# Linear attention and a mixture of experts on one core: the first batch's loads and steps in a new order

## The chip, the core and the metric

The kernel runs on one core of a Trainium2 chip. A core has a matrix engine (TensorE, PE in the profile, with PEld for its weight loads), VectorE (DVE), ScalarE (ACT), GpSimd (POOL) and SyncE (SP). Each engine works through its own list of instructions in order and waits on semaphores for the others. Transfers from memory are issued by SP, ACT or POOL and carried by 16 DMA engines: queue 1 in the profile holds what SP issues, queue 10 what ACT issues, queue 0 what POOL issues. The metric is device time in microseconds (us) of one execution; the figure compared is the median of several runs.

## What is computed

Linear attention over 8 batches of 8 heads, 576 tokens and head size 64, and then a mixture of 4 experts over the 4608 tokens:

```
phi(x) = where(x > 0, x, exp(x) - 1) + 1
kv  = einsum('bhsd,bhde... over s', phi(k), v)        # 64 x 64 per head
z   = sum over s of phi(k)
x   = (phi(q) @ kv) / (phi(q) . z + 1e-6)             # heads side by side: 4608 x 512
p   = domain_probs / (sum of domain_probs + 1e-9)     # 4608 x 4
out = sum over e of p[:, e] * (relu(x @ w1[e]) @ w2[e])   # w1[e]: 512 x 1024, w2[e]: 1024 x 512
```

All inputs are float32 in memory; the matrix products run on float16.

## The kernel before

**Tiles.** The tokens are cut into nine tiles of 512. Tile j below 8 holds the first 512 tokens of batch j; the ninth collects the 64 tokens left over in each batch. For each tile the attention makes x, which is transposed to xT, and then four experts follow, each with a layer 1 (x times w1, relu) and a layer 2 (times w2, scaled by p and added up in `acc`). The products are done in a form that saves multiplications (`Block` and `layer2_product`, with sums of weights, of tokens and of hidden values made on DVE and POOL). Only expert 0 of tile 0 is done plainly, by `layer1_half` and `layer2_part`.

**Batch 0.** Its attention stands at the start of the kernel, when nothing else can run, and has a class of its own, `First` (lines 558 to 666). Its k and v come in four pieces of two heads (288 KB each), its q in four pieces of 256 KB: pieces 0 and 1 are the first token half, pieces 2 and 3 the second half, of heads 0 to 3 and 4 to 7. In memory a row of a q piece is 512 bytes long, a row of a k or v piece 2304 bytes. The steps, by the names that the order uses, with i the number of the piece:

- `lq`, `lk`, `lv`: loads, issued on SP or ACT as the settings `LQ`, `LK`, `LV` say; `lpr0`: the first probabilities
- `ke`, `kl`, `km` (lines 582 to 590): exp of k on ACT, max(k + 1, 1) on the engine that `KL` names, their minimum on DVE; `qe`, `ql`, `qm` (lines 599 to 607): the same for q
- `vc` (line 593): v cast to float16 on the engine that `VC` names
- `kv` (line 626): 18 matmuls on PE and two copies of the result, on engines that `KC` names
- `qT` (line 615): four transposes of q on PE and a copy on ACT
- `nd` (line 648): numerators and denominators on PE, a reciprocal and a product on DVE; the first digit is the pair of head pairs, the second the token half
- `xT` (line 662): two transposes of x on PE and a copy on ACT or DVE; first digit the pair of heads, second the token half
- `L` (line 675): layer 1 of expert 0 for two of the eight column blocks and one token half, in two parts (heads of pairs 0 and 1, then of pairs 2 and 3)
- `warm` (line 1016): matmuls on zeros, whose result nobody reads; `WARM` has their numbers

**Weights and batch 1.** They are loaded by POOL (`load_second`), which converts weights to float16 on the way: `w100` is layer 1, expert 0, piece 0, and so on; `k0`, `v2`, `q1` are pieces of batch 1, `rk0`, `rv1` its leftover tokens. The sums of weights are `s` and `t`, the sums of tokens `ts`, the products of the later experts `p1` to `p7`, `c22` and `y`.

**The order.** Nothing is scheduled by the machine. Each step is a generator that records its instructions; the list `EARLY` (lines 103 to 135) is read from left to right and each name advances its step by one part. Instructions go to the lists of their engines in the order in which they are recorded. What comes after `EARLY` runs by positions in other settings. `BANK` says which pair of PSUM banks a step uses, and so which earlier step has to be done with it. Raw pieces of q, and of batch 1, share six buffers (`praw`, line 220). A transfer also waits until the one that used its semaphore before has landed.

Of the kernel before, what the change touches and what calls it, by code (L numbers as in the profile page):

```python
# [90 lines left out]
    "LK": 'ASSS',  # L91
    "LV": 'SSSS',
    "KL": 'VVVV',
    "VC": 'PVAP',
    "QL": 'VVPV',
    "QT": 'AAAA',
    "KC": ('AA', 'AV', 'VA', 'AA'),
    "XT": ('AA', 'AA', 'AV', 'AV'),
    "CUT": (((0, 2, 4),) * 4, ((0, 2, 4),) * 4),
    "MOVE": {"m73.10": 512.0, "m73.11": 512.0, "m73.20": 512.0, "m73.21": 512.0, "m72.41": 528.0},  # L100
    "WARM": (14, 3, 2, 1, 5),
    "BANK": {'qT0': 'py', 'qT1': 'b', 'nd00': 'py', 'nd00+': 'b', 'kv2': 'py', 'xT00': 'b', 'kv3': 'b', 'nd10+': 'b', 'L00': 'b', 'L10': 'py', 'nd01': 'b', 'xT01': 'py', 'nd11+': 'b', 'L20': 'e', 'L30': 'e', 'L01': 'e', 'L11': 'py', 'L21': 'py', 'L31': 'b', 'b1.qT3': 'py', 'b1.nd30': 'py', 'b1.nd21': 'b', 'b1.q1': 'b', 'b1.qT1': 'py', 'b1.nd01': 'py', 'b1.xT2': 'b', 'b1.nd11': 'py', 'b1.xT0': 'b'},
    "EARLY": (
        "lq2 lq3 lq0 lk0 qe0 ql0 ql3 qm0 kl0 lk1 lpr0 ke0 km0 qe2 ql2 qm2 lv0 ke1 kl1 km1 warm0 qT0 lv1 lk2 qe3 qm3 warm1 qT2 qT0 vc0 w100 warm2 kv0 vc1 qT2",
        "warm3 kv1 lk3 kv0 kv0 kl2 kv1 kl3 w102 kv1 nd01 lv3 nd01 warm4 xT11 xT01 ke2 km2 qT3 w103 vc3 lv2 ke3 vc2 nd00 w101 km3 xT01 w110 xT11 w111 kv3 k3 kv2",
        "qT3 lq1 nd00 qe1 xT00 w200 kv3 rk1 ql1 kv3 kv2 w201 qm1 L01 kv2 nd11 xT10 L31 qT1 v0 nd11 rv0 xT00 xT10 L10 xT21 rk0 xT21 v1 xT31 L11 qT1 xT31 nd10",
        "L01 L01 rv1 L31 w120 nd10 ts0.2 L00 ts0.0 xT30 ts0.1 xT20 L31 s0.0 L20 xT20 L30 xT30 L10 L10 L00 L00 L30 ts0.3 L30 p1.011 s1.0 p1.010 L11 L20 p1.010",
        "p2.010 s1.1 L20 w121 p2.010 p1.011 L21 L21 L21 s1.2 p6.010 p5.010 w210 L11 s1.3 p6.011 y0.30 p2.011 p6.010 p7.010 w211 p7.010 s0.1 p6.011 c22.010 v2",
        "y0.31 y0.00 p4.010 p2.011 y0.32 y0.33 p5.011 b1.k3 k0 pr0 y0.33 t0.0 t0.1 b1.km3 p7.011 p7.011 c22.011 y0.01 y0.02 y0.03 p4.010 b1.lk y0.20 y0.03 k2",
        "p4.011 s0.2 p3.010 p4.011 p3.011 y0.21 y0.10 y0.22 p3.010 y0.11 b1.v0 q1 k1 p1.021 y0.23 p1.021 p3.011 p1.020 s2.0 y0.12 v3 p2.021 b1.lv p1.020 t0.3",  # L110
        "s2.1 p2.020 s2.3 s2.2 y0.23 b1.v1 q0 t0.2 p6.020 p6.020 y0.13 p6.021 y0.13 y1.20 p7.020 y1.21 p2.020 p5.020 p7.020 w130 p2.021 y1.22 y1.23 t1.0 y1.10",
        "w131 p5.021 b1.v2 q3 b1.lkm y1.11 p6.021 b1.k0 b1.k2 b1.k1 w220 t1.1 t1.2 p7.021 y1.12 p7.021 c22.020 p3.020 y1.23 b1.v3 b1.km0 p4.020 p4.020 y1.00",
        "y1.01 q2 w221 y1.13 p4.021 b1.km2 b1.km1 b1.kv c22.021 p3.021 y1.02 y1.03 p1.030 p4.021 b1.q1 y1.30 y1.13 b1.load1 p1.031 b1.q0 p3.020 y1.31 p3.021",
        "p1.030 b1.qm1 b1.qT1 y1.32 y1.03 b1.qm0 s3.0 p1.031 w231 b1.qT0 s3.1 p2.030 y1.33 p6.030 b1.kv b1.qT0 p6.031 p2.031 b1.nd00 b1.nd01 b1.q3 p6.030 s3.3",
        "y1.33 p7.030 b1.loadlq p2.030 p5.030 b1.qm3 b1.qT3 p6.031 p7.030 w230 b1.qT1 b1.nd01 p7.031 p4.030 b1.qT3 s3.2 c22.030 b1.nd10 b1.nd11 b1.nd00 p2.031",
        "p3.030 b1.nd11 b1.nd10 p7.031 y2.00 y2.01 b1.nd30 p5.031 p4.031 p4.030 b1.next b1.nd31 b1.nd30 y2.20 b1.load0 b1.xT0 b1.lq b1.lqm b1.nd31 b1.q2 b1.qm2",
        "y2.21 b1.xT3 y2.02 c22.031 p4.031 b2.load2 y2.03 s0.3 b1.xT3 b1.qT2 y2.22 y2.23 b2.load1 b1.xT1 b1.load4 b1.load3 b1.load2 lpr b1.qT2 b1.nd20 p3.031",
        "b1.xT1 p3.030 b1.nd21 y2.03 b1.xT0 b1.nd20 b1.nd21 y2.23 y2.10 y2.11 ts1.0 p1.101 p1.101 b1.load5 t1.3 b2.load0 t2.0 b1.xT2 y2.12 y2.13 b1.xT2 b2.k1",
        "ts1.1 y2.30 y2.31 p1.100 p1.100 y2.32 y2.33 p3.031 p2.101 y3.20 y2.13 b2.km1 p6.100 b2.lk p2.100 t3.0 b2.load4 p2.101 p6.101 p6.100 p2.100 b2.lv",
        "ts1.2 p7.100 ts1.3 p7.100 b2.k0 y3.21 p5.100 y2.33 y3.22 t2.1 p4.100 y3.23 p6.101 p5.101 p4.100 p7.101 y3.30 c22.100 p3.100 b2.ones b1.qTl b2.v3 y3.00",  # L120
        "y3.01 p7.101 p4.101 b2.k2 b2.lkm y3.23 b2.km0 b2.load3 c22.101 b2.v1 y3.31 p3.100 t2.3 y3.32 p4.101 hs10.00 p3.101 b2.load5 y3.02 p1.110 b2.km2 y3.33",
        "p3.101 y3.03 b2.k3 b2.v0 b2.km3 b2.v2 b2.kv p1.110 y3.33 b2.load10 m10.21 b2.load7 p1.111 y3.03 y3.10 hs10.01 b1.qTl b2.q0 y3.11 p6.110 hs10.10",
        "hs10.02 y3.33 pr1 y3.12 y3.03 p1.111 m10.21 b2.q3 b2.load11 b2.qm0 y3.13 m10.51 hs10.11 p2.110 p6.111 p6.110 b2.q2 p2.111 m10.51 b2.qm3 y3.13 p2.110",
        "p6.111 t2.2 p7.110 m10.11 p5.110 m10.20 p7.110 b2.qm2 m10.11 b2.q1 c22.110 hs10.03 hs10.12 p7.111 m10.61 b2.qm1 t3.1 m10.20 p4.110 p4.110 p3.110",
        "p3.110 m10.50 p1.120 t3.2 b1.nl p2.111 p5.111 b3.load1 hs10.13 m10.61 m10.31 m10.31 m10.50 m10.10 p7.111 p4.111 b2.kv hs11.00 m10.10 m10.71 p1.120",
        "c22.111 t3.3 p6.120 m10.71 b2.lq b2.lqm p4.111 m10.60 b1.nl hs11.01 p3.111 p1.121 p6.120 y3.13 b2.load6 b2.qT m10.41 b2.qTl m10.60 m10.30 p2.120",
        "b2.nd1 p3.111 m10.41 m10.30 p7.120 b2.nd1 b2.nd0 hs11.10 y3.23 m10.70 m10.70 m11.21 hs11.11 p2.120 p5.120 m11.21 m10.40 p7.120 p4.120 hs11.03 p1.121",
        "p6.121 m11.20 m11.51 c22.120 p3.120 m10.40 b2.nd0 m11.20 p4.120 b3.k1 m11.50 m11.51 b3.km1 m11.11 p6.121 p2.121 m11.50 b2.nd1 b2.nd2 p3.120 p7.121",
        "m11.11 b2.nd3 b2.nd2 p1.130 hs11.02 p7.121 hs12.00 p2.121 b3.load0 b2.nd3 hs11.13 m11.10 m11.10 b2.next m11.61 m11.61 p5.121 p1.130 c22.121 p2.130",
        "m11.60 m11.31 p3.121 p6.130 m11.31 p4.121 b2.nd3 p6.130 hs11.12 m11.71 p4.121 p3.121 hs12.01 hs12.02 p2.130 m11.60 b2.nd4 hs12.10 p7.130 m11.71",  # L130
        "hs12.12 b2.nd5 p7.130 b2.nd2 b2.load8 m11.30 p5.130 p1.131 p1.131 m11.41 ts2.0 b2.nd4 b2.nd5 b2.nd5 m11.30 m11.41 m11.70 hs12.03 p6.131 p6.131 m12.20",
        "m11.70 m11.40 hs12.11 b3.ones c22.130 p4.130 p3.130 b1.xl p7.131 m12.21 p4.130 p7.131 m12.20 m11.40 b2.nl p2.131 b3.v0 p1.200 m12.21 b2.nl m12.50",
        "p2.131 m12.50 m12.51 p4.131 hs12.13 m12.51 ts2.1 p3.130 m12.10 m12.10 m12.11 m12.11 p5.131 p1.200 ts2.3 m12.60 m12.61 ts2.2 m12.60 b3.k0 m12.61",
        "c22.131 hs13.00 b2.load9 p4.131 p6.200",
    ),
}

# [1032 lines left out]
```

## Time and profile before

| what | value |
|---|---|
| median of 3 runs | 485.64 us (484.6 to 485.81) |
| the profiled execution | 484.06 us, of which the span of the core's instructions 482.3 us |
| TensorE busy | 474.5 us (98%) |
| VectorE, ScalarE, GpSimd busy | 377.6, 331.4, 356.1 us |
| granted TensorE clock | 1.0 |
| bytes moved by DMA | 53.67 MB, mean 111 GB/s |
| the same up to 60 us, in slices of 12 us | 218 to 292 GB/s |

The span runs from the first to the last instruction of the program. Busy time counts an engine as busy while an instruction of its own runs; matmuls are pipelined, so their ends overlap the next one's start. A chain is the work that ended last, followed back step by step to what released it. The time from issue to landing of a transfer includes its wait behind others. In a line of a stretch of time the columns are: the stretch, its length, busy time and number of instructions of PE, PEld, DVE, ACT and POOL, the granted clock, the busy share of the DMA engines, and GB/s.

### The profile page before, as it was taken

What the parts mean: (1) busy time and instruction counts of PE and PEld (TensorE: products, weight loads), DVE (VectorE), ACT (ScalarE), POOL (GpSimd) and SP (SyncE); (2) the same over time, 40 slices, a digit from 0 to 9 for tenths busy, and PEclk for the clock granted to TensorE, in tenths of its full rate; (3) what the DMA queues carried; (4) which work ended last, traced back from release to release, by engine and by line L of the source; (5) the groups of instructions that cost most, each with busy time, mean ns of one, the idle gap of its engine ahead of it and who ended that gap; (6) DMA issues with size and microseconds to landing.
All of it is one profiled execution on the core that took longest, in us unless ns stands there. A gap on an engine that the chain in (4) does not pass through costs nothing.

```text
span 482.3 us, 12013 instructions
## 1 busy us (share of the span) xinstructions
PE 474.5 (98%) x4565; PEld 407.4 (84%) x4565; DVE 377.6 (78%) x794; ACT 331.4 (69%) x662; POOL 356.1 (74%) x340
## 2 busy tenths in 40 slices
PE   7999999999999999999999999999999999999997
PEld 3766766898889888998889888988898888888886
DVE  5778988997868895889679885988787756775677
ACT  4689989956895599649874888478954465446540
POOL 5566044789866986789777977697769877987775
PEclk9999999999999999999999999999999999999999
DMA  8999986442445154533552436323230020003002
GB/s 292 219 218 256 232 212 210 124 112 83 135 140 115 39 160 154 119 59 117 173 134 62 112 123 170 78 73 112 65 68 12 2 88 2 0 1 89 2 1 87
DMA packets 80025, 53.67 MB, mean 111 GB/s; under 512 B 45088, under 2 KB 72736, under 8 KB 79968
## 3 DMA queue, kind: packets, MB, share of 16 engines
q1 hardware_dynamic: 69920, 40.56, 30.6%
q0 software_dynamic: 8800, 11.27, 12.1%
q10 hardware_dynamic: 1248, 1.08, 0.7%
q8 instruction: 35, 0.57, 0.5%
q14 instruction: 22, 0.18, 0.1%
HBM read 45.16 MB, written 9.44 MB: 113 GB/s over the span
## 4 chain that ended last, share of the span: by engine, by line
PE 96%; DVE 1%; DMA 1%; issue 0%; ACT 0%; SPq 0%; DVEq 0%
PE py L830 39%; PE pb L887 25%; PE pe L887 19%; PE py L735 6%; PE ph L675 1%; PE psum_nd L492 1%; PE psum_kv L464 1%; DMA rawq<-in_q_dram 1%; PE pb L830 1%; PE pe L830 1%; DVE kpos L586 0%; PE psum_nl L510 0%; PE psum_num L648 0%; PE psum_xh L662 0%; DVE qp L607 0%
## 5 line engine op out<-in xcount | busy, mean ns | idle before, releaser
L726 DVE SCALAR_TENSOR_TENSOR acc<-py,p_sb,acc 128x256 f32<-128x256 f32 (+1 forms) x382 | 182.3, 489 | 42.3 <-PE py L830 38.3
L871 DVE CUSTOM_DVE_ANT_0 h<-pe,u 128x512 f16<-128x512 f32 x140 | 96.2, 689 | 45.5 <-PE pe L887 27.8
L887 PEld LDWEIGHTS <-w 128*128 128x128 f16 x1120 | 108.9, 98 | 16.2
L797 POOL TENSOR_TENSOR hs<-h 128x512 f16<-128x512 f16 x64 | 74.6, 1165 | 56.9 <-DVE h L871 52.8
L830 PEld LDWEIGHTS <-h 128*128 128x128 f16 x1024 | 99.6, 98 | 11.5
L830 PE MATMUL py<-w,h 128*128 128x256 f16 x744 | 106.4, 273 | 0.0
L898 ACT COPY u<-pb 128x512 f32<-128x512 f32 x140 | 82.5, 592 | 29.9 <-PE pb L887 27.8
L799 POOL TENSOR_TENSOR hs<-hs,h 128x512 f16<-128x512 f16 x64 | 73.9, 1155 | 26.3 <-PE py L830 23.8
L887 PEld LDWEIGHTS <-s 128*128 128x128 f16 x840 | 81.2, 98 | 12.0 <-DVE s L767 0.2
L887 PE MATMUL pb<-tt,w 128*128 128x256 f16 x560 | 83.9, 273 | 0.0
L830 PEld LDWEIGHTS <-hs 128*128 128x128 f16 x768 | 74.5, 98 | 8.8 <-issue 0.2
L803 POOL TENSOR_TENSOR hs<-h,hs 128x512 f16<-128x512 f16 x64 | 74.4, 1162 | 0.9 <-PE py L830 0.7
L830 PE MATMUL py<-t,hs 128*128 128x256 f16 x496 | 74.1, 273 | 0.0
L801 POOL TENSOR_TENSOR h<-h 128x512 f16<-128x512 f16 x64 | 73.9, 1154 | 0.1
L920 ACT ACTIVATE h<-pe 128x512 f16<-128x512 f32 x70 | 42.0, 601 | 41.3 <-PE pe L887 40.7
L913 ACT COPY pe<-pb 128x512 f32<-128x512 f32 x70 | 40.0, 572 | 42.0 <-PE pb L887 15.8
L941 ACT ACTIVATE h<-pb 128x512 f16<-128x512 f32 x70 | 41.9, 601 | 6.0 <-PE pb L887 5.9
L887 PE MATMUL pe<-tt,s 128*128 128x256 f16 x280 | 42.0, 273 | 0.0
L887 PE MATMUL pb<-tt,s 128*128 128x256 f16 x280 | 41.8, 273 | 0.0
L887 PE MATMUL pe<-xT,s 128*128 128x256 f16 x248 | 37.1, 273 | 0.0
L887 PE MATMUL pb<-xT,w 128*128 128x256 f16 x248 | 37.1, 273 | 0.0
L830 PE MATMUL py<-w,hs 128*128 128x256 f16 x248 | 37.0, 273 | 0.0
(132 smaller groups left out, 594.4 us busy)
## 6 DMA issues: line engine op xcount, KB each, us to landing
w<-in_moe_w_dram POOLq DMA_DIRECT2D x14, 512.0 KB, 10.6
out_dram<-acc SPq DMA_DIRECT2D x28, 256.0 KB, 2.6
rawb<-in_k_dram SPq DMA_DIRECT2D x24, 256.0 KB, 3.0
rawb<-in_q_dram SPq DMA_DIRECT2D x24, 256.0 KB, 2.7
rawb<-in_v_dram SPq DMA_DIRECT2D x24, 256.0 KB, 2.7
out_dram<-acc SPq DMA_DIRECT2D x12, 128.0 KB, 2.4
w<-in_moe_w_dram POOLq DMA_DIRECT2D x4, 256.0 KB, 5.5
rawb<-in_k_dram POOLq DMA_DIRECT2D x4, 256.0 KB, 10.4
```

The lines of the kernel that those rows point to most:

```text
L726: nc.vector.scalar_tensor_tensor(out=acc, in0=ps, scalar=pscal, in1=acc, op0=AO.mult, op1=AO.add)
L797: nc.gpsimd.tensor_tensor(out=hs[0], in0=a21, in1=a22, op=AO.add)
L799: nc.gpsimd.tensor_tensor(out=hs[1], in0=hs[0], in1=a11, op=AO.subtract)
L801: nc.gpsimd.tensor_tensor(out=a21, in0=a11, in1=a21, op=AO.subtract)
L803: nc.gpsimd.tensor_tensor(out=hs[3], in0=a12, in1=hs[1], op=AO.subtract)
L830: nc.tensor.matmul(out=ps, lhsT=lhsT(k), rhs=rhs[:, k], start=first and k == 0, stop=k == FH - 1, skip_group_check=True,)
L871: nc.vector._custom_dve(TENSOR_ADD_SAT, out=out, in0=ps, in1=u, s0=BIG, s1=0.0)
L887: nc.tensor.matmul(out=ps[:, kk], lhsT=lk(kc), rhs=rhs[:, kc], start=first and kk == 0 and kc == 0, stop=kc == 1, skip_group_check=True,)
L898: nc.scalar.copy(u, self.b)
L913: nc.scalar.copy(self.e5, self.b)
L920: nc.scalar.activation(self.h[:, :, 0, 0:NH], self.e5, AF.Relu)
L941: nc.scalar.activation(self.h[:, :, 1, 0:NH], self.b, AF.Relu)
```

## The change

Only settings change; no function does.

- SP's list of loads was q2, q0, k1, probabilities, v0, v1, k2, k3, v3, v2, q1. It becomes q2, v0, k1, v1, k2, v2, k3, v3, q0, q1, probabilities. ACT issues q3 and k0 as before.
- POOL had max(q + 1, 1) of piece 2, the casts of v0 and v3, and issued the first piece of w after the cast of v0. Now it casts v0, issues `w100`, casts v1 and issues `w102`, `w103`, `w101` and the rest. All four max(q + 1, 1) are on DVE, the casts of v2 and v3 on ACT.
- ACT and DVE begin with q pieces 2 and 3 and then k; q pieces 0 and 1 come after k is done.
- Layer 1 of expert 0 began with column blocks in both token halves. Now the second token half is begun in all column blocks (`L01 L11 L31 L21`) before the first half of the tokens.
- PSUM banks of the steps of batch 0 are given out anew; the warm matmuls are 21 and not 25.
- The rest of `EARLY`, up to tile 1, has the same steps in a new order; weights and batch 1's pieces are loaded in nearly the order of before, with the pieces of batch 1 at other places among them.

```diff
-    "VC": 'PVAP',
-    "QL": 'VVPV',
+    "VC": 'PPAA',
+    "QL": 'VVVV',
     "QT": 'AAAA',
-    "KC": ('AA', 'AV', 'VA', 'AA'),
+    "KC": ('AA','AV','VA','AA'),
     "XT": ('AA', 'AA', 'AV', 'AV'),
...
-    "WARM": (14, 3, 2, 1, 5),
-    "BANK": {'qT0': 'py', 'qT1': 'b', 'nd00': 'py', 'nd00+': 'b', 'kv2': 'py', 'xT00': 'b', 'kv3': 'b', 'nd10+': 'b', 'L00': 'b', 'L10': 'py', 'nd01': 'b', 'xT01': 'py', 'nd11+': 'b', 'L20': 'e', 'L30': 'e', 'L01': 'e', 'L11': 'py', 'L21': 'py', 'L31': 'b',
+    "WARM": (13, 3, 2, 1, 2),
+    "BANK": {'qT3': 'py', 'kv1': 'py', 'nd01': 'py', 'kv3': 'py', 'xT11': 'py', 'nd11': 'py', 'xT31': 'py', 'nd00': 'py', 'qT1': 'py', 'xT10': 'py', 'nd10': 'py', 'xT30': 'py', 'L01': 'e', 'L11': 'e', 'L21': 'b', 'L31': 'b', 'L00': 'e', 'L10': 'e', 'L20': 'b', 'L30': 'b',
...
     "EARLY": (
-        "lq2 lq3 lq0 lk0 qe0 ql0 ql3 qm0 kl0 lk1 lpr0 ke0 km0 qe2 ql2 qm2 lv0 ke1 kl1 km1 warm0 qT0 lv1 lk2 qe3 qm3 warm1 qT2 qT0 vc0 w100 warm2 kv0 vc1 qT2",
-        "warm3 kv1 lk3 kv0 kv0 kl2 kv1 kl3 w102 kv1 nd01 lv3 nd01 warm4 xT11 xT01 ke2 km2 qT3 w103 vc3 lv2 ke3 vc2 nd00 w101 km3 xT01 w110 xT11 w111 kv3 k3 kv2",
-        "qT3 lq1 nd00 qe1 xT00 w200 kv3 rk1 ql1 kv3 kv2 w201 qm1 L01 kv2 nd11 xT10 L31 qT1 v0 nd11 rv0 xT00 xT10 L10 xT21 rk0 xT21 v1 xT31 L11 qT1 xT31 nd10",
-        "L01 L01 rv1 L31 w120 nd10 ts0.2 L00 ts0.0 xT30 ts0.1 xT20 L31 s0.0 L20 xT20 L30 xT30 L10 L10 L00 L00 L30 ts0.3 L30 p1.011 s1.0 p1.010 L11 L20 p1.010",
...
+        "lq2 lv0 lq3 lk0 lk1 lv1 qe2 qe3 lk2 lv2 ql3 ql2 vc0 w100 vc1 qm3 qm2 warm0 lk3 ke0 qT2 warm1 kl0 lv3 w102 km0 kl1 w103 qT2 ke1 w101 w110 w111 rv0 kv0",
+        "qT3 km1 qT3 kv0 kv0 ke2 warm2 kv1 kl2 kv1 ke3 vc2 vc3 kv1 kl3 km2 nd01 w200 nd01 warm3 rv1 w201 k1 rk0 kv2 k2 w120 k3 xT11 xT01 lq0 lq1 qe0 ql0 km3",
+        "ql1 qm0 kv2 warm4 kv3 rk1 lpr0 w121 w210 v2 k0 w211 v0 v1 v3 q1 qe1 kv2 xT11 kv3 kv3 xT01 nd11 q2 w130 qm1 qT1 qT0 L01 L11 qT1 w131 w220 q0 qT0 w221",
+        "nd11 nd00 xT21 L31 xT31 L21 nd00 q3 xT21 xT31 nd10 xT00 xT10 L21 L01 xT10 L21 xT00 nd10 xT30 L31 xT20 xT30 L01 L11 L30 xT20 L30 L20 L20 L10 L10 L00",
...
```

(The lines of the list that follow, up to tile 1, have the same steps in another order; it ends with the same steps.)

## The prediction

> **What bounds the kernel now.** I read the page first (span, busy time, slices, chain), then busy time by stage, then the chain of the first 20 us, then the DMA queues stretch by stretch. From the page:
>
> ```profile
> span 482.3 us, 12013 instructions
> PE   7999999999999999999999999999999999999997
> ...
> PE 96%; DVE 1%; DMA 1%; issue 0%; ACT 0%; SPq 0%; DVEq 0%
> ```
>
> TensorE (PE) is the bound. Busy time by stage (us, then PE, PEld, DVE, ACT, POOL, granted clock, DMA share, GB/s) says where it is not:
>
> ```profile
> 8.00:12.00 4.00, 2.71 (x49) 1.42 (x48) 3.90 (x8) 2.81 (x8) 3.98 (x6) 1.00 1.09 367
> 12.00:16.00 4.00, 2.99 (x62) 2.04 (x62) 3.20 (x9) 3.17 (x8) 4.00 (x7) 1.00 1.24 205
> 16.00:20.00 4.00, 4.00 (x52) 3.54 (x53) 2.75 (x9) 2.09 (x8) 1.91 (x3) 1.00 1.15 212
> 20.00:60.00 40.00, 40.00 (x346) 29.03 (x344) 33.43 (x66) 36.31 (x74) 15.84 (x22) 1.00 1.18 236
> 60.00:480.00 420.00, 418.71 (x4043) 369.06 (x4041) 331.08 (x698) 283.98 (x565) 327.36 (x294) 1.00 0.34 93
> ```
>
> From 16 us on PE never rests. So the change is worth what it does to one moment, the start of that unbroken stretch at 15.98 us, provided no hole appears behind it. What sets that moment, from the chain (start, us, what):
>
> ```profile
> 1.25 4.94 DMA rawq<-in_q_dram
> ...
> 6.22 0.64 ACT ee L601
> ...
> 11.12 1.24 DVE kpos L586 x2
> ...
> 15.23 0.70 DVE x_sb L652
> ...
> 15.98 0.28 PE psum_xh L662 x2
> ```
>
> A q piece landing at 6.20 lets ACT and DVE begin; they carry the chain to the x that PE transposes at 15.98. DMA, the third resource, is full from the start. First query, 8.3 to 11.4 us: queue 1 holds SP's loads. Second, 8.3 to 9.2: the first piece of w, 4.9 us to landing. Third, 52 to 54: POOL's queue 0 beside queue 1.
>
> ```profile
> q1 hardware_dynamic: 889, 1.19, 105.6%
> ```
>
> ```profile
> w<-in_moe_w_dram POOLq DMA_DIRECT2D x1, 256.0 KB, 4.9
> ```
>
> ```profile
> q0 software_dynamic: 310, 0.36, 94.0%
> q1 hardware_dynamic: 309, 0.08, 28.8%
> ```
>
> Until 11.4 us queue 0 moves nothing, though w is issued from 8.38: in this kernel the first loads and w hardly meet. When both queues have work (310 packets against 309, and 90 against 87 in 49.5 to 50.5) they take turns packet by packet, whatever the sizes.
>
> **The parts.**
>
> *Fewer warm matmuls* (25 to 21): they stand before waits, worth nothing. The clock matters: the first twelve take up to 634 ns, from 5.9 us on 376 to 393.
>
> *Earlier start.* q pieces 2 and 3 feed ACT and DVE first; piece 2 lands at 4.25, not 6.20 (SP's first load, issued 0.74, 3.5 us). Behind them the loads have the same bytes, so I keep the landings' spacing of 0.75 us per 288 KB and 0.65 per 256 KB: k0 and v0 6.1, k1 6.85, v1 7.6, k2 8.35, v2 9.1, k3 9.85, v3 10.6, q0 11.25, q1 11.9. Adding rows down ACT's list (exp 0.62 to 0.67, the next starting 0.55 later; qT copies 0.60; kv copies 0.21; v casts 0.66): k exp 6.15, copies of kv0 end 8.9, that of kv1 9.66, k exp 3 ends 10.55, v casts 11.65, q exps 12.75. Down DVE's (q lin and min 0.42, k lin 0.45 to 0.68, reciprocal 0.21, norm 0.69): kv1's copy 9.9, k min 2 11.0, first x 11.85, q lin 12.25, k min 3 12.65, then the lin of q1.
>
> *From there everything hangs on q1.* DVE's list is: lin q1, min q0, copy kv2, min q1; ACT's: exp q1, copy kv2, xT, two copies of kv3, xT, two qT copies. PE's next steps (numerators of pairs 2 and 3, two turns, then layer 1) wait for those. If q1 can be used at T: kv2 copied T+1.25, last kv3 copy T+1.95, numerators T+2.0, turn of q0 T+2.4, layer 1 T+2.6, and 0.13 lost before the next numerators, which wait for the last qT copy at T+3.55. At T+2.4 the same 1.57 us of small matmuls is left as before at 15.98 (6 transposes of x at 0.11, 2 numerators at 0.34, a turn at 0.23). So the change is T + 2.53 − 15.98 = T − 13.45, with T at least 12.55, when DVE gets there. With q1 at 11.9 it is −0.9.
>
> *The POOL queue is the catch.* Before, POOL does a q lin (1.92 us from 4.33) and a v cast at 7.76, and issues w at 8.38. After, its list is cast v0, w, cast v1, w, w, w: v0 lands at 6.1, the cast takes 0.66, so w is issued at 6.8, 1.6 us earlier, while v3, q0 and q1 still queue (before, q1 was ahead of w). First packet of w: 3.0 us after the issue as before gives 9.8; a newcomer behind large packets takes longer (SP's k load issued at 44.52: no packet of queue 1 before 48.1, 3.6 us), which gives 10.4; with half a us more, 10.9. I take 10.4: the engines then hold large packets too. From then on a q packet goes with each packet of w. q pieces are 512 packets of 512 B, 32 per engine; a pair takes 2 us × 16 / 310 = 0.103 us, against 0.02 for a q packet alone (0.65/32). At 10.4 some 57 are left, 5.9 us: q1's data ends at 16.3, T = 16.7 with the 0.35 from last packet to landing. Bounds: w at 9.8 leaves 64 and part of v3, T = 17.75; at 10.9 about 40, T = 15.1. w has four pieces of 16 packets per engine in that stretch, so the pairing doesn't run dry.
> [...]
>
> *Price:* T − 13.45 = +3.25 (+1.6 to +4.3).
>
> *Later order.* w comes in nearly the same order and DMA stays full, so landings move little. Counting PE's work on from layer 1 at T+2.6, the second half of w2 of expert 2 is needed 41.9 us later. It landed at 58.8 before (need 60.4); one q piece (0.65) now comes after it: 58.15. With T = 16.7 the need is at 61.2: no wait. With T = 12.55 it is at 57.0: 1.15 us of wait that takes the gain back. The probabilities' 8 KB go from fourth to last on SP; the first py is scaled some 14 us after layer 1 begins, which covers them. SP now issues q1 into the buffer of q piece 2, after that one's exp and lin; those end by 5.5, and SP is at q1 no sooner than 6.1, when k0, whose semaphore it also waits for, lands. On POOL, batch 1's k pieces 1 and 2 go ahead of w1 of expert 2 (0.65 each): it lands near 32.9 and is needed 19.1 us after layer 1 begins, 34.2 at the earliest. Casts and banks are charged nothing: DVE 33.4 and ACT 36.3 of 40 us (20 to 60) have room for what moves: a v cast from POOL to ACT (0.66), a q lin from POOL to DVE (0.42) against a v cast from DVE to POOL (0.75); without that cover they cost up to 1.1.
>
> **Sum.** The profiled execution took 484.06 us, span 482.3 and 1.76 around it; the runs' median, 485.64, is 1.58 above it. 484.06 + 3.25 = 487.31; as a median, 488.9. A change below 0.3% (1.46 us) can't be told from none.
>
> **The rivals.**
>
> *A. q delayed by w, clock kept:* 488.9 (487.2 to 490.0). Against it: no row shows w starting while SP's queue is full; w's first packet at 11.4 comes just as SP's loads end, which also fits a newcomer that stands behind all of them.
>
> *B. The same, and PE's clock falls.* PE would do kv3 at about 14.5 and nothing until 18.3. Before, its longest idle stretch once warm is 0.77 us. Cold, the first 4.7 us (1.2 to 5.9) ran at half rate; again, that costs 2.35: 491.2. [...] No row here shows a fall within the kernel.
>
> *C. w stays behind all SP loads as before* (not slower). T = 12.55, −0.9, 484.7. Place: the DMA engines at 9.8 to 11; it decides if T stays under 13.45. With the wait for w2 it is +0.2: 485.8. If w also streams 1.6 us earlier the wait is gone and the gain stays, at most some 1.6 with my walk off by 0.7.
>
> *D. Partial sharing,* T from 13 to 14.9: −0.45 to +1.45, 486.1.
>
> **Numbers.** A 0.45, B 0.13, C 0.28, D 0.14. Slower: A, B and a little of D, 0.60. Faster by over 0.3% only in the best of C, raised a little for errors in my walk, 0.12. The rest 0.28. Predicted is A's 488.9, its own range 487.2 to 490.0. The range goes from C's 484.7 to B's 491.2, leaving out C's better end and B's worse.
>
> **What would show it.** In the changed kernel: w first issued near 6.8; queue 1 sharing packets with queue 0 from about 10.4; q0 and q1 landing near 13.4 and 16.7, the latter 10 us after its issue and not 5; ACT's exp of q1 and DVE's lin waiting for that DMA; PE dense from about 19, none of it waiting for w. Wrong if q1 lands near 12 (C), if matmuls of layer 1 start 0.22 us apart instead of 0.11 (B), or if PE waits for DVE or ACT between 20 and 110 us, where the order is new and many of its inputs were ready only 0.05 to 0.3 us ahead.

## The result, and the profile after

The changed kernel takes 490.0 us (median of 6 runs, 489.35 to 490.43) against 484.34 us for the kernel before, measured beside it (483.96 to 485.81): a ratio of 1.0108, interval 1.009 to 1.0125. The profiled execution took 489.61 us, with a span of 487.8 us against 482.3 before.

From the page of the changed kernel, the span, TensorE's slices, the granted clock in slices, and the shares of the chain:

```profile
span 487.8 us, 12000 instructions
...
PE   7899999999999999999999999999999999999997
...
PEclk9799999999999999999999999999999999999999
...
PE 90%; DMA 4%; ACT 2%; DVE 2%; issue 1%; ACTq 0%; SPq 0%; DVEq 0%
```

PE is still the bound, but its second slice (12 to 24 us) is no longer full, the granted clock has a 7 in that slice where full speed is 9, and the chain holds 4% of DMA (20 us) where it held 1%.

Busy time by stage shows the clock more closely. The stretches are cut to where the clock changes in the changed kernel (columns: stretch, length, PE, PEld, DVE, ACT, POOL, granted clock, DMA share, GB/s). First the changed kernel, then the same cut of the kernel before, whose matmuls come up to full speed at the same 5.9 us:

```profile
5.90:9.30 3.40, 3.14 (x52) 1.59 (x51) 2.90 (x6) 2.58 (x6) 2.96 (x5) 1.00 1.05 402
9.30:12.70 3.40, 1.54 (x36) 1.10 (x31) 2.29 (x7) 3.31 (x7) 3.40 (x6) 1.00 1.15 287
12.70:16.10 3.40, 2.19 (x29) 1.31 (x28) 1.91 (x6) 1.59 (x6) 2.13 (x3) 0.51 1.28 211
16.10:19.60 3.50, 3.50 (x33) 3.00 (x31) 0.90 (x2) 1.37 (x3) 1.35 (x2) 0.51 1.16 211
19.60:23.00 3.40, 3.40 (x42) 2.85 (x41) 2.82 (x8) 1.56 (x5) 0.71 (x1) 1.00 1.14 216
```

```profile
5.90:9.30 3.40, 2.01 (x14) 0.79 (x13) 2.98 (x7) 3.08 (x6) 1.90 (x3) 1.00 1.05 404
9.30:12.70 3.40, 2.13 (x48) 1.26 (x46) 3.19 (x7) 2.21 (x7) 3.38 (x6) 1.00 1.13 316
12.70:16.10 3.40, 3.07 (x63) 2.12 (x63) 2.71 (x7) 2.58 (x7) 3.40 (x6) 1.00 1.24 205
```

From 9.3 to 12.7 us PE is busy for 1.54 of 3.40 us (45%) and right behind that the clock is halved for 6.8 us; before, it was busy for 2.01 us (59%) in the stretch from 5.9 and for 2.13 us (63%) in this one, and the clock stayed. Counted from the moment at which the warm matmuls come up to full speed (5.91 us), the changed kernel's clock falls 6.83 us later, at 12.73, and comes back after another 6.83, at 19.56; in experiment 6 the two times are 6.83 and 3.42, in experiment 7 about 3.4 and 10.2. All are close to whole multiples of 3.41, and a stretch of that length, counted from that moment, is called a window below. No stretch of 3.4 us is empty: PE's longest pause behind 2 us is 1.21 us, and that one, the wait for q1, comes at 14.5, when the clock is down already. The first matmuls of layer 1 are the slowed ones (changed kernel, timeline; start, duration, engine, line, what):

```profile
17.12 1.92 PE L675 MATMUL ph<-xT,w 128*128 128x256 f16 x8
```

Eight take 1.92 us with the end of the last, and 1.04 us at full speed (experiment 8, below). The chain, which counts from start to start, has 1.71 us for eight here and 0.87 for eight from 21.34 on: 0.21 apart against 0.11.

The delay at the start is in the chain of the first 18 us of the changed kernel (start, duration, what):

```profile
1.26 4.84 DMA kraws<-in_k_dram
...
6.21 7.83 DMA rawq<-in_q_dram
...
14.50 0.14 DVE qp L607
...
15.31 0.38 ACT xT L664
...
17.33 0.85 PE ph L675 x4
```

q1, issued at 6.21, lands at 14.05, 7.83 us later, and everything up to layer 1 hangs on it. Its neighbour on the queue, q0, lands at 11.28, undisturbed. POOL's issue is the other side (timeline), and the queues from 11 to 13 us show them together (packets, MB, share):

```profile
6.35 0.87 POOL L244 DMA_DIRECT2D w<-in_moe_w_dram  x1
```

```profile
q0 software_dynamic: 280, 0.27, 80.4%
q1 hardware_dynamic: 379, 0.17, 40.2%
```

Asking for w 2 us sooner brought nothing: it lands at 13.44, before at 13.30.

Behind 20 us PE waits again, in places that had no wait before. The waits of PE from 20 us on (us in total, times, longest), and a piece of the chain from 78 to 106 us:

```profile
PE py L830 <- ACT acc L724: 0.9, 2, 0.5
PE py L830 <- DVE acc L726: 0.4, 1, 0.4
```

```profile
82.05 4.88 DMA rawb<-in_q_dram
86.95 0.63 ACT qp L364
```

A q piece of batch 2, which SP now issues at 82.05 (the same piece before: 78.03), lands at 86.9, and ACT, which works through its list in order, stands for 0.70 us until then.

To see where the 5.5 us of span went, I add up from each moment on the matmuls still to be done at full speed, warm ones left out, in both traces. The changed kernel is behind by 1.9 us at 20 us, 2.65 at 60, 3.7 at 90, 4.9 at 120 and 5.6 at the end: a third in the head, the rest in several smaller steps behind it. The experiments take these apart.

### The profile page after: what moved, and what is told of

Its sections match the earlier page's. It is cut to its first block, busy times and chain, and to the rows that moved or that the text cites. A ratio compares the mean times of both kernels' runs of the same rounds, so it can differ in the third digit from the quotient of the medians.

```text
span 487.8 us, 12000 instructions
## 1 busy us (share of the span) xinstructions
PE 478.0 (98%) x4561; PEld 409.0 (84%) x4561; DVE 377.4 (77%) x794; ACT 332.8 (68%) x663; POOL 354.6 (73%) x339
## 3 DMA queue, kind: packets, MB, share of 16 engines
q0 software_dynamic: 8800, 11.27, 11.9%
## 4 chain that ended last, share of the span: by engine, by line
PE 90%; DMA 4%; ACT 2%; DVE 2%; issue 1%; ACTq 0%; SPq 0%; DVEq 0%
PE py L830 37%; PE pb L887 24%; PE pe L887 18%; PE py L735 5%; DMA rawq<-in_q_dram 2%; PE ph L675 2%; PE psum_nd L492 1%; DMA rawb<-in_q_dram 1%; DMA kraws<-in_k_dram 1%; PE psum_kv L464 1%; PE pb L830 1%; DVE acc L726 1%; DMA xT<-x_sb 1%; PE pe L830 1%; DVE h L871 1%
```

## The experiments

Ratios are to the kernel before, measured beside each: 484.74 us in experiments 1 to 4, 484.58 in 5 to 8, 484.39 in 9 and 10. Kernel 3 is the kernel of experiment 3, and so on.

**1. w asked for after v1's cast.** One entry of the list, changed kernel:

```diff
-... lv2 ql3 ql2 vc0 w100 vc1 qm3 qm2 warm0 ...
+... lv2 ql3 ql2 vc0 vc1 w100 qm3 qm2 warm0 ...
```

> The changed kernel with one swap on POOL: the cast of v1 ahead of the first piece of w, so that w is issued near 8.4 us as before and not at 6.35. Theory A (the last q loads are slowed by w, which takes turns with them): q1 lands near 12.0 instead of 14.05, and PE begins layer 1 near 15.2 instead of 17.1. Rival K (only the fallen clock costs, the late q1 is harmless): q1's landing may move, the time does not. For the whole both have a part: the clock fell at 12.7 because of the idle time between 9.3 and 12.7, which this edit does not touch, so it should fall here too, and PE then does up to 4 us of dense work at half rate. Expected: q1 at 12.0 in the trace, clock 0.5 from 12.7 to 16.1 or 19.6; time 0 to 1.5 us below the changed kernel's 490.0.

Measured 488.65 us, 1.0076 (1.0064 to 1.0089). w is issued at 8.48, q1 lands at 12.03 and not at 14.05, w at 13.34. So the mixing is the cause of q1's delay, but not of the fallen clock. The profiled execution, 487.42, was the fastest of five, and in it the clock never fell; the other four (488.33 to 488.79) have mean clocks of 0.992 to 0.996. Same instructions, other outcome. PE's busy time in the stretch before the danger point, with the clock full from 6.85 us in this execution:

```profile
10.27:13.68 3.41, 2.12 (x47) 1.30 (x46) 3.11 (x9) 2.94 (x6) 3.41 (x5) 1.00 1.22 255
```

2.12 of 3.41 us (62%), and the clock holds. Yet the same trace, cut from 9.32 to 12.74 us as the window lay in the changed kernel, has only 1.56 of 3.42 us (46%). In the twelve profiled executions of this case the warm matmuls come up to full speed at anything from 4.5 to 7.2 us, and the windows, counted from there, lie at other moments of the kernel accordingly. That this made the difference among the five is my reading; where the windows lay in the other four was not recorded.

**2. More warm matmuls**, w left early. 34 in place of 21, the new ones around kv2 and kv3:

```diff
-    "WARM": (13, 3, 2, 1, 2),
+    "WARM": (13, 3, 2, 3, 4, 2, 7),
...
-... rk0 kv2 k2 ... kv2 warm4 kv3 rk1 ...
+... rk0 kv2 warm5 k2 ... kv2 warm4 kv3 warm6 rk1 ...
```

> The changed kernel with 12 more matmuls on zeros in the idle time of PE before layer 1 (3 instead of 1 before kv2, 2 after it, 4 instead of 2 before kv3, 7 after it), w issued early as in the changed kernel. Theory K: the granted clock stays 1.0 between 12.7 and 19.6, and 1.3 to 1.8 us of the 5.6 go: 488.4. q1 still lands near 14. Rival (the clock's fall lay beside waiting and cost nothing): clock 1.0 and 490.0. [...]

Measured 487.73, 1.0069 (1.0056 to 1.0083): 2.3 us under the changed kernel although q1 lands even later, at 14.26. The clock is 0.999 to 1.0 in all five executions. At 20 us this kernel is 0.81 us behind the kernel before, where the changed kernel is 1.9 behind; so 1.1 of the 2.3 us are saved in the head itself, and the rest in waits behind it.

**3. Both.** The step of 1, and warm matmuls (13, 3, 2, 3, 3, 2, 4) in the places of 2.

> Both edits: w after the cast of v1, and 8 more matmuls on zeros. If A and K together are all of the loss up to 30 us, PE's unbroken stretch begins as early as my sum for an undisturbed start had it (0.9 us ahead of before), and the time is 2.6 to 3.3 us below the changed kernel, near 487.0; what is left over before's 484.3, some 2.7 us, then lies behind 60 us. If the time is near 484, the later losses were only consequences of the head.

Measured 486.43, 1.0036 (1.0023 to 1.0048). Against 2 that is 1.3 us less, the price of the mixed queues (it also has four warm matmuls fewer). Against 1 it is 2.2 us less, of which the clock explains about half: 1's one execution with the clock up took 487.42, still 1.0 above. In that execution the late q piece of batch 2 takes 5.52 us to land (4.82 here, below), and PE waits 1.05 us behind it where it waits 0.35 here; why it takes longer is not shown. With q1 at 12.00 the head is 0.3 us ahead of the kernel before at 20 us by the sum of what is left, and yet the kernel ends 1.7 us later than it: something behind the head costs 2 us. Its chain still has the late q piece:

```profile
79.69 4.82 DMA rawb<-in_q_dram
84.53 0.63 ACT qp L364
```

**4. The kernel before up to 68 us, the changed order behind.** The first 396 entries of the list are those of the kernel before, and what is left comes in the changed kernel's order; all other settings are those of before.

> The kernel before, its first 396 entries of the order (to some 68 us), then the changed kernel's order for all later entries. Theory L (the new order behind 68 us costs by itself: ACT waits at 82 us for a q piece of batch 2): 2 to 3 us above before, 486.3 to 487.3, with PE gaps between 80 and 120 us. Rival (those gaps come from what the changed head left late): within 0.5 us of before, 484.3.

Measured 485.85, 1.0025 (1.0017 to 1.0034). The late order costs 1.1 us by itself. In its profiled execution, the fastest of eleven, PE has no wait between 20 and 95 us and two holes behind, at 100.78 and 115.68. The waits of PE from 20 us on:

```profile
PE pb L887 <- ACT h L941: 0.4, 1, 0.4
PE py L830 <- DVE acc L726: 0.4, 1, 0.4
```

**5. The converse.** Kernel 3 up to 68 us (398 entries), then the order of before.

> The head, and everything up to about 68 us, in the changed kernel's order, with w asked for after v1's cast and the extra warm matmuls (as in the run that measured 486.43); from there the order of the kernel before. Theory: about 1.1 us of the loss belongs to the late part of the order (the q piece of batch 2 that is asked for late, and the hole near 100 us), the rest to the first 60 us: some 485.3, and PE without a hole over 0.3 us near 85 and near 100 us. Rival: the holes come from work that the early part leaves late, whatever order follows: 486.4 again, with the holes at the same places. Second rival: the early half's other choices of banks cost by themselves; then 485.9 with no hole over 0.2 us.

Measured 486.07, 1.0035 (1.0022 to 1.0047). A miss for all three: the late order of before doesn't mend it, and the holes aren't where they were. They are now at 69.70 (0.84 us) and 76.94 (0.44 us):

```profile
PE pe L887 <- ACT pe L913: 0.8, 1, 0.8
PE py L735 <- DVE acc L726: 0.4, 1, 0.4
```

So the loss behind the head isn't in the late part alone. Here the holes stand right behind the seam at 68 us; in experiment 4 they come 30 to 50 us behind it. That each half of an order fits the half it was made with is a reading that both allow and neither shows; whether a single entry carries the loss isn't shown either.

**6. w asked for ahead of every cast**, in the changed kernel:

```diff
-... lv2 ql3 ql2 vc0 w100 vc1 qm3 ...
+... lv2 ql3 ql2 w100 vc0 vc1 qm3 ...
```

> The changed kernel with one step moved: POOL asks for the first piece of w ahead of its cast of v0, so at about 5.6 us and not at 6.35. This is a larger dose of the same mixing of the two queues. Theory: the first packets of w come as much earlier as it is asked for (about 10.1 and not 10.9), more of q1's packets are paired with packets of w, q1 lands at 14.9 to 16 and not at 14.05, and the time is above the changed kernel's by what q1 is later, so 490.5 to 492. Rival: w only starts when SP's queue has nothing more waiting ahead of it, so its first packet stays at about 10.9, q1 at 14.05 and the time within 0.3 us of 490.0.

Measured 488.26, 1.0075 (1.0061 to 1.0089): 1.7 us *less* than the changed kernel, and a miss for both. I had overlooked that nothing stands ahead of w on POOL then: it is issued at 1.37 us and not at 5.6, and meets the loads at their beginning. It lands at 9.05. Every later load is 1.3 us behind its undisturbed landing (v1 8.83, k2 9.68, q0 12.58), but q1, at 13.34, is sooner than with w issued at 6.35: the second piece of w isn't asked for until 9.49. So it isn't true that the sooner w is asked for the worse: at 6.35 the whole delay falls on the one piece that everything waits for. The clock fell here too, for one window (stretches cut to it, columns as above):

```profile
9.83:13.24 3.41, 1.71 (x46) 1.28 (x41) 2.53 (x7) 2.80 (x6) 3.41 (x6) 1.00 1.12 350
13.24:16.66 3.42, 3.08 (x40) 2.20 (x38) 2.23 (x8) 2.20 (x8) 3.22 (x6) 0.50 1.25 209
16.66:20.07 3.41, 3.41 (x46) 2.81 (x45) 1.98 (x7) 1.04 (x3) 0.93 (x2) 1.00 1.13 210
```

PE was busy for 50% of the window ahead of it. So a part of the 1.7 us is the clock, at half speed for one window and not for two. The five executions show the price within one program: 487.23 with a mean clock of 1.0, 487.87 to 488.27 with 0.996 (one window), 488.82 with 0.993 (two).

**7. The kernel before with fewer warm matmuls.** The clock in the other kernel, by itself:

```diff
-    "WARM": (14, 3, 2, 1, 5),
+    "WARM": (14, 1, 1, 1, 1),
```

> The kernel before with fewer warm matmuls: 14, 1, 1, 1, 1 and not 14, 3, 2, 1, 5. Nothing else is changed. Theory: the clock falls after a stretch in which PE is busy for about half of the time, so that without these seven matmuls the busy share between 9 and 16 us goes from 63 per cent towards 45, the clock falls in some or all of the executions, matmuls after 16 us start 0.24 us apart for up to 7 us, and the time is 1 to 2.3 us above the kernel before, or spread between the two. Rival: warm matmuls before waits are worth nothing, as the prediction charged them: within 0.3 us of the kernel before, with the clock at full speed throughout.

Measured 487.05, 1.0046 (1.0033 to 1.0059), with clocks of 0.989 to 0.993 in all five executions. Seven matmuls of which nobody reads the result are worth 2.5 us. In the trace 1.9 us of the delay are there at 20 us, where the clock is back; another 1.1 arise far behind, the larger part of it at two waits of PE for ACT at 142 and 193 us, and why these come is not shown. The fall came one window sooner than I thought, after 43% busy:

```profile
5.90:9.30 3.40, 1.47 (x11) 0.53 (x10) 2.93 (x7) 3.04 (x6) 1.91 (x3) 0.99 1.05 404
9.30:12.70 3.40, 3.09 (x46) 1.94 (x46) 3.25 (x7) 1.87 (x6) 3.37 (x6) 0.50 1.14 317
12.70:16.10 3.40, 2.78 (x37) 2.18 (x38) 1.93 (x6) 2.58 (x7) 3.40 (x6) 0.50 1.23 204
```

**8. The mended head, then the order of before.** Kernel 3 up to the end of layer 1 (its casts, banks and steps, 160 entries, POOL's loads in the order of before), and from there the entries of before.

> Batch 0's attention in the changed order (k and v ahead of two q pieces, w asked for after v1's cast, the extra warm matmuls), then layer 1 onward in the order of the kernel before. Theory: the head by itself gains about 0.3 us, which is all that the head of the mended kernel showed at 20 us, and nothing behind it waits: 484.4 against 484.7, too little to be told from none. Rival: layer 1 in before's column order wants tokens that the changed head makes last, so PE waits near 17 us and the time is 485.5 or more.

Measured 484.30 (11 runs), 0.9996 (0.9987 to 1.0004): the same as before. It is 2.1 us under kernel 3, whose head it shares but for the order of POOL's loads. So the changed order of POOL's loads, or of the steps behind layer 1, or both, cost these 2.1 us; the two were not run apart. The casts and banks of batch 0, which this kernel shares with the changed one, cost nothing that shows. At 20 us it is 0.36 us ahead; at 26.69 and just behind it gives back 0.5, because the order of before finds ACT a little later there. The only wait of PE behind 20 us:

```profile
PE pe L887 <- ACT h L920: 0.3, 1, 0.3
```

**9. That hole taken on.** In kernel 8, the last part of one of layer 1's steps (`L00`) and its activation go behind the next product's matmuls and activation:

```diff
-... p1.010 L00 p1.011 L31 ... p1.010 L00 s0.0 p2.010 p2.010 p1.011 p6.010 ...
+... p1.010 p1.011 L31 ... p1.010 p2.010 L00 s0.0 p2.010 L00 p1.011 p6.010 ...
```

> The kernel that measured 484.30 (mended head, then the order of before) with one hole taken on: at 26.69 us PE waited 0.31 us for ACT to read a bank, and here the last quarter of layer 1 and its activation are put behind the matmuls whose bank ACT has to free. Theory: the head keeps its 0.3 us and the hole is gone, 484.0, about 0.6 under the kernel before and just enough to be told from it with five rounds. Rival: the hole moves to the next bank, 484.3 or more.

Measured 485.03 (12 runs), 1.0013 (1.0004 to 1.0023): the rival. One hole of 0.31 us became two, each for a bank that ACT still reads:

```profile
PE pb L887 <- ACT pe L913: 0.5, 1, 0.5
PE pe L887 <- ACT pe L913: 0.3, 1, 0.3
```

No version here beats the kernel before.

**10. The mixed queues by themselves.** Kernel 8 with w asked for between the casts of v0 and v1, as in the changed kernel.

> The kernel that measured 484.30 with one step put back to where the changed kernel has it: POOL asks for the first piece of w between the casts of v0 and v1, 2 us sooner. The order after layer 1 is that of the kernel before, so the price of the mixed queues is seen by itself. Theory: q1 lands near 14.1 and not 11.98, PE is 1.1 to 1.3 us later at 20 us, nothing gives it back, and the clock stays up because the extra warm matmuls are there: 485.4 to 485.6; if the longer wait lets the clock fall all the same, 487 to 488. Rival: the delay of q1 was paid for in the changed kernel only through its later order: within 0.3 us of 484.3.

Measured 485.51 (11 runs), 1.0022 (1.0013 to 1.0031): 1.2 us above kernel 8, as expected. q1 lands at 14.11; the clock stays (0.999 to 1.0 in all eleven). From its chain of the first 18 us:

```profile
6.29 7.83 DMA rawq<-in_q_dram
```

## Why the prediction was right, and where it was wrong

The time lies in the range and 1.1 us from the forecast, and slower was forecast and came. The mechanism that was charged, q1 held up behind w, is there; but it is a small part of the time, and that the sum came so near is luck. From the changed kernel to kernel 8, which equals the kernel before, the runs go 490.0, 487.73 (clock mended), 486.43 (w later), 484.30 (POOL's loads and the order behind layer 1 as before):

| term | predicted | measured by these steps |
|---|---|---|
| head without w's interference | −0.9 (T = 12.55) | −0.3 at 20 us, −0.2 in the end |
| q1 behind w | +4.15 (T = 16.7) | +1.3; +1.2 by experiment 10 |
| the clock | 0 (rival B: 2.35) | +2.3 |
| later order (with POOL's loads) | 0 | +2.1 |
| sum | +3.25 | +5.5 |

Two terms that I left out came to 4.4 us, and the two that I charged, 3.25, came to 1.1. These steps are differences of medians; by the ratios, each to the kernel before measured beside it, the clock comes to 1.9 us, w to 1.6 and the order to 1.9. Nor is each term spent where it arises. At 20 us the changed kernel is 1.9 behind: T − 13.45 with q1 at 14.05 makes 0.6 of it, the clock the other 1.3. The other 3.7 arise behind 20 us. What is lost there differs from trace to trace: 2.4 us in kernel 3's and 3.6 in kernel 1's, both with q1 in time and the clock up, and why is not shown.

The forecast also stood on a median of before of 485.64, over 0.9 us above those measured later (484.34 to 484.74).

- *PE is the bound and the change is worth what it does to the start of the unbroken stretch, provided no hole appears behind.* The first half held. The proviso didn't: 2.1 us of holes.
- *T − 13.45.* It held where q1 is late and the clock is up: with q1 at 14.11 (experiment 10) it gives +0.66, and at 20 us that kernel is 0.66 behind the one before; with 14.26 (experiment 2) +0.81 against 0.8.
- *T at least 12.55, when DVE gets there.* The undisturbed landings were right to 0.1 us (q0 11.25 predicted, 11.28 measured; q1 11.9 and 12.0). But DVE gets to q1 at 13.04 (kernel 8's timeline), so the undisturbed gain is 13.04 − 13.45, some −0.4, against −0.3 measured and −0.9 predicted. What was off is my walk down DVE's list, half a us short over 6 us:

```profile
13.04 0.42 DVE L604 TENSOR_SCALAR qp<-rawq 128x512 f16<-128x512 f32 x1
```

- *w's first packet at 10.4, some 57 packets of q left, T = 16.7.* The mis-sized term. w was issued at 6.35, even sooner than the 6.8 that I worked out, but its packets begin at about 10.9 (8 packets of queue 0 between 10 and 11 us, 280 between 11 and 13): 4.5 us after the issue, where I had taken 3.6 from SP's load at 44.5 us and 4.1 as the bound. By then q0 had its data, and only q1 was left to share. 10.9 was in my bounds, but with about 40 packets left and T = 15.1, and that was summed wrongly: from 57 at 10.4, at my own 0.02 us a packet, 32 are left at 10.9, and T is 14.5. q0 was indeed through, 32 were left, and they took 2.8 us (10.9 to 13.7, where the data ends if the last 0.35 are as I had them), 0.088 a pair and not 0.103. By the size, this was rival D (T 13 to 14.9), which I gave 0.14. Rival C, where w stays behind all of SP's loads, is out: q1 landed 2 us late.
- *Rival B, the clock falls: price 2.35.* It fell. That the step to kernel 2 is 2.3 us looks like my price, but is chance: I priced matmuls at half speed in the head (warm ones start 0.43 us apart before 5.9 us and 0.22 behind), and these cost 1.3 us at 20 us; within one program two windows cost 1.2 to 1.6 (experiments 1 and 6). I made the fall hang on 3.8 us without a matmul while q1 is awaited, and gave it 0.13. That such a pause brings the clock down was an assumption that no run shows. Its cause was another: it fell at 12.7, ahead of that wait, because 1.54 us of matmuls in the 3.4 before were too few, and it fell in four executions of five with q1 in time (experiment 1). Experiment 7 shows the same after 1.47, experiment 6 after 1.71, while 2.01 and 2.13 (before) and 2.12 (experiment 1) kept it: here the boundary lies between 50% and 59%. Slid over the traces of experiments 2, 3, 5, 8, 9 and 10, a stretch of 3.41 us that starts between 5 and 15 us is nowhere under 65% busy, and none of their 49 executions has a mean clock under 0.998. The kernel before is nearer the edge: of the 23 executions beside experiments 9 and 10 two have a clock of 0.996, and they took 485.70 and 485.75, 1.3 above the median. No fall had a window without matmuls ahead of it: the three that preceded one held 1.47 to 1.71 us of them.
- *Fewer warm matmuls stand before waits, worth nothing.* Wrong: thirteen more gain 2.3 us (experiment 2), seven fewer cost 2.5 (experiment 7), counting the waits behind the head in both. They fill waits: with the thirteen the mean clocks were 0.999 to 1.0, without the seven 0.989 to 0.993. Whether the four that the change took out would have been enough was not run.
- *Later order, casts and banks charged nothing.* Right for casts and banks of batch 0 (experiment 8). Wrong for the order, POOL's loads or the steps: 2.1 us. I had looked at whether weights land in time, and they did: no wait of PE for w shows, and the 1.15 us for w2 of expert 2 that I feared with an early T is not in kernel 3, whose hindmost waits are for ACT and DVE. What I named as a risk in the last sentence, inputs that are ready only 0.05 to 0.3 us ahead, is what happened, without a price. Still open is which entries do it: experiments 4 and 5 show that neither half of the order is free of it.

## What to carry to other kernels

A stretch in which the matrix engine waits cost more here than the wait itself, once a window of 3.41 us was only half busy (45% in the changed kernel, with the clock halved for 6.83 us behind it): count the matmuls of every stretch of that length, the useless ones too, before you take any out. An early request was no gain where it only made the queues take turns sooner (w, issued at 6.35 us, landed at 13.44, and at 13.34 when issued at 8.48), and it did harm where the piece on the critical path was the last in the other queue (q1 at 14.05 against 12.03); ask who shares with whom at the moment the data starts to flow. An order written by hand is easily spoilt: exchanging a part of it or moving a few steps (experiments 4, 5 and 9) left two waits of PE of 0.3 to 0.8 us each, together more than the 0.3 us that the head was able to gain.

## What the runs showed of the hardware

- The clock fell after windows in which PE was 43, 45 and 50% busy, and held after 59, 62 and 63%. Once fallen, it came back after one window in experiment 6 (3.42 us), after two in the changed kernel (6.83) and after three in experiment 7 (about 10.2). In experiment 7 a window with 3.09 us of half-speed matmuls out of 3.40 did not bring it back, though 3.08 out of 3.42 did in experiment 6. So PE's busy time in the profile does not by itself tell when the clock comes back.
- The first piece of w, which POOL issued at 6.35 us while SP's queue was full, waited 4.5 us for its first packets (at about 10.9, changed kernel; from 10 to 11 us queue 1 moved 659 packets and queue 0 eight). Issued at 1.37, ahead of most of SP's loads (experiment 6), it held the later ones up by 1.3 us (q0 landed at 12.58 against 11.28). Issued at 8.48, behind them (experiment 1), it landed at 13.34, as soon as when issued at 6.35 (13.44).
